# Three PSUM banks for the block products, and another order of weight sums, input sums, splits and norms

## The chip, the cores and the metric

One core of a Trainium2 chip runs the program. The metric is the device time of one execution in microseconds (us); lower is better. Engines in the text: PE (TensorE, matrix products), PEld (its weight loads), DVE (VectorE), ACT (ScalarE), POOL (GpSimd), SP (the engine that issues most of the DMAs).

## The reference

A layer norm of x, 32-head attention on it (q, k, v from one 512 x 1536 matrix), a squared-ReLU feed-forward whose SiLU gates the attention's output, and a residual. S = 2048 tokens, D = 512, 32 heads of 16, F = 1792, all float32.

```python
def _A_ref(x, wqkv, wo):
    qkv = (x @ wqkv).reshape(B, S, 3, H, Dh)      # -> q, k, v per head
    p = softmax(q @ k.T * Dh ** -0.5)
    return (p @ v).reshape(B, S, D) @ wo

def _B_ref(x, w1, b1, w2, b2):
    h = relu(x @ w1 + b1) ** 2
    return h @ w2 + b2

xn = layernorm(x)
out = x + _A_ref(xn, A_wqkv, A_wo) * silu(_B_ref(xn, B_w1, B_b1, B_w2, B_b2))
```

## The kernel before

The order of all work is written by hand: each engine runs its instructions in the order in which the program issues them, and a tile framework adds the semaphore waits that the tiles' reads and writes call for.

**Stages.** The tokens come in four chunks of 512 (`NC = 4`). The first part of the span, up to about 176 us, makes v, k and q of all chunks; the rest is one long loop over heads and key blocks (scores on L381, exponentials on L385, values on L699, the feed-forward's products on L429 between them). This case is about the first part.

**Precision.** Each float32 operand is split in two parts of a reduced format, high (a cast) and low (the difference, L104 or L298). A product takes three of the four combinations: high-high, high-low, low-high.

**A chunk.** `norm` (L159) normalizes two token tiles at a time: statistics (L166, L172), a square root on ACT (L176), three small DVE operations (L179 to L181), and the normalization (L186). `transposes` (L214) turns a chunk on PE (L201) into two PSUM tiles S0 and S1, ACT copies the high part (L205), DVE makes the low part (L211), and four sums of input quarters follow (L228, L231). `split_sums` (L234) splits those four sums: 0 and 3 with POOL, 1 and 2 with DVE. Then four value tiles of 12 matmuls each (`linear`, L111) are copied by ACT into `vt` (L655), and four groups g of keys and queries follow.

**Chunk 0** makes keys and queries directly (`keyquery`, L273: 12 matmuls of 512 columns into a rotating S tile, an ACT cast L98, a DVE subtraction L104, one DMA). Between its groups stand the four weight sums (`weight_sum`, L286, on DVE, L290, in place in the raw weight tiles) and their splits (`split_weight_sum`, L293: a cast on ACT, L296, and two subtractions on POOL, L298).

**Chunks 1 to 3** make keys and queries of a group together, as a 2 x 2 block product with seven products in place of eight (`fast_keyquery`, L314). A product is six matmuls of 256 columns (L324). The seven use input quarters, the four input sums (x sums, tags u0, u1, y0, y1), weights, and the four weight sums. ACT copies the first product out as r (L331) into `tmp`, which lies in the tile QA1; that tile held the raw weights from which weight sum 3 is made. DVE adds the products up (L327), and ACT and DVE and POOL make high and low parts (L343, L351, L352, L354). Two DMAs on SP write keys and queries. Before, the products go round four banks:

```python
    four_banks = t([128, 2, 512], FT, "S2")
    four_banks = [t([128, 512], FT, "lin"), four_banks[:, 0], four_banks[:, 1], t([128, 512], FT, "acc")]
```

so banks two and three are halves of one tile, and the value tiles go to them first: `four_banks[(1, 2, 3, 0)[i]]`.

**Chores.** DVE's add in `fast_keyquery` may be followed by one step of a generator, `chores`: the transposes, low parts and input sums of the next chunk, one step behind every third add. The norms of the next chunk run among the value tiles.

**PSUM.** Eight banks: S0, S1, S2 of two banks each, `lin` and `acc`.

Of the kernel before, what the change touches and what calls it, by code (L numbers as in the profile page):

```python
# [24 lines left out]
FT = mybir.dt.float32  # L25
FR = mybir.dt.float32r
I32 = mybir.dt.int32
AF = mybir.ActivationFunctionType
OP = mybir.AluOpType
# [44 lines left out]
def fast_path(tc, sb, ps, env):  # L74
# [7 lines left out]
    dve, act, pool, sp = nc.vector, nc.scalar, nc.gpsimd, nc.sync  # L82
# [3 lines left out]
    def t(shape, dt, tag):  # L86

        cnt[0] += 1
        p = ps if tag in ("S", "S0", "S1", "S2", "lin", "acc") else sb
        if tag in BUFS:  # L90
            turn[tag] = turn.get(tag, -1) + 1
            n = turn[tag] % BUFS[tag]
            tag = f"{tag}{places[n] if tag == 'S' else n}"
        return p.tile(shape, dt, tag=tag, name=f"{tag}_{cnt[0]}")
# [7 lines left out]
    def split(hi, lo, src, heng, leng):  # L102
        cast(heng, hi, src)
        leng.tensor_tensor(lo, src, hi.bitcast(FT), op=OP.subtract)  # L104
# [9 lines left out]
    def run(gen):  # L114
        for _ in gen:
            pass
# [10 lines left out]
    def load_x(c):  # L127
        for i in range(2):
            a = xload[c, i] = t([128, 2, 512], FT, f"P{4 + 2 * (c == 1) + i}")
            r = c * 512 + i * 256  # L130
            sp.dma_start(a, x[r:r + 256].rearrange("(a p) d -> p a d", p=128))
            if c == i == 0:
                load_w("v", sp, (0,))
# [100 lines left out]
    def split_sums(c, which, eng):  # L234
        for j in which:
            tag = ("u0", "u1", "y0", "y1")[j]
            xs4[j] = t([128, 2, 2, 256], FR, tag)
            split(xs4[j][:, 0], xs4[j][:, 1], xsum[c][j], act, eng)
# [47 lines left out]
    def weight_sum(j):  # L286

        (k0, k1), (q0, q1) = wraw["k"], wraw["q"]
        dst, u, v = ((k0, q0, k0), (q1, q1, k0), (q0, q1, q0), (k1, q1, k1))[j]
        dve.tensor_tensor(dst, u, v, op=OP.subtract)  # L290
        return dst

    def split_weight_sum(j, h, l):  # L293

        src = wraw[("k", "q", "q", "k")[j]][(0, 1, 0, 1)[j]]
        act.copy(h, src)  # L296
        for k in range(2):
            pool.tensor_tensor(l[k], src[:, k], h[:, k].bitcast(FT), op=OP.subtract)  # L298
        ws4[j] = [h[:, 0], h[:, 1]], l
# [12 lines left out]
        return lambda p, k: wsp[which][p][2 * j + k][:, s]  # L312

    def fast_keyquery(c, g, banks, chores, tags, tmp):  # L314
        one, two, three, four = (b[:, :256] for b in banks)
        r, u2, u3 = (tmp[:, j] for j in range(3))
        kk, qq = (t([128, 2, 512], FT, tag) for tag in tags)
        khi, qhi, klo, qlo = (e[:, p].bitcast(FR) for p in range(2) for e in (kk, qq))

        def product(dst, xn, wn, more=False):  # L320
            xp, wp = x_part(c, xn), w_part(wn, g)
            todo = [(k, a, b) for a, b in ((0, 0), (0, 1), (1, 0)) for k in range(2)]
            for n, (k, a, b) in enumerate(todo):
                mm(dst, wp(a, k), xp(b, k), start=n == 0 and not more, stop=n == 5, skip_group_check=True)  # L324

        def add(dst, u, v, op=OP.add):
            dve.tensor_tensor(dst, u, v, op=op)  # L327
            next(chores, None)

        product(one, (0, 0), ("k", 0))  # L330
        act.copy(r, one)  # L331
        product(two, 2, 2)
        add(u2, two, r)
        product(three, 3, 3)
        add(u3, three, u2)
        product(four, 1, 1)
        add(qq[:, 1, 256:], four, u3)
        if (c, g) == (3, 3):
            turn["S"] = -1
            first = [scores(0, p) for p in range(2)]  # L340
            exps(0, 0, first[0])
        product(one, (0, 1), ("k", 1), more=True)
        act.copy(khi[:, :256], one)  # L343
        if (c, g) == (3, 3):
            exps(0, 1, first[1])
        add(klo[:, :256], one, kk[:, 0, :256], OP.subtract)
        product(two, (1, 1), 4)
        add(kk[:, 1, 256:], u3, two, OP.subtract)
        product(four, 4, ("q", 1), more=True)
        add(qq[:, 1, :256], four, u2)  # L350
        act.copy(khi[:, 256:], kk[:, 1, 256:])  # L351
        act.copy(qhi, qq[:, 1])  # L352
        add(klo[:, 256:], kk[:, 1, 256:], kk[:, 0, 256:], OP.subtract)
        pool.tensor_tensor(qlo, qq[:, 1], qq[:, 0], op=OP.subtract)  # L354
        sp.dma_start(kdram[g][c // 2][:, :, 512 * (c % 2):512 * (c % 2) + 512], kk)
        sp.dma_start(qdram[g][c], qq)
# [26 lines left out]
    def exps(i, p, src):  # L383
        if src is not None:
            act.activation(ptile[i, p], src, AF.Exp, scale=SCALE)  # L385
# [184 lines left out]
    parts = [norm(0, (0,)), norm(0, (1,)), norm(0, (2, 3))]  # L570
# [28 lines left out]
    def chain(*gens):  # L599
        for g in gens:  # L600
            yield from g

    parts = chain(norm(1, (0, 1)), norm(1, (2, 3)))
# [5 lines left out]
    for g in range(4):  # L609
        if g == 1:  # L610
            bp = t([128, 14], FT, "acc")
            nc.tensor.transpose(bp, b1raw, ident[:14, :14])
            dve.tensor_copy(b1t, bp)
        if g == 3:
            prep = transposes(1)
            for _ in range(3):
                next(prep)
            save_xT(1)
        for which in "kq":
            keyquery(0, g, which, ("lin", "acc")[which == "q"] if g == 3 else "S")  # L620
            next(parts, None)
            if (g, which) == (1, "q"):
                weight_sum(0)
                a = t([128, 2, 2, 512], FR, "KA2")
                split_weight_sum(0, a[:, 0], [a[:, 1, k] for k in range(2)])
            if (g, which) == (2, "k"):
                weight_sum(2)
                weight_sum(1)
                split_weight_sum(1, t([128, 2, 512], FR, "gl"), [t([128, 512], FR, "ou") for _ in range(2)])
            if (g, which) == (2, "q"):  # L630
                weight_sum(3)
        if g == 0:
            load_x(2)
    h, l = (t([128, 2, 512], FR, f"P{6 + p}") for p in range(2))
    split_weight_sum(2, h, [l[:, 0], l[:, 1]])
    run(prep)

    four_banks = t([128, 2, 512], FT, "S2")
    four_banks = [t([128, 512], FT, "lin"), four_banks[:, 0], four_banks[:, 1], t([128, 512], FT, "acc")]
    tmp = t([128, 4, 256], FT, "QA1")  # L640
    for c in range(1, NC):
        split_sums(c, (1, 2), dve)
        split_sums(c, (0, 3), pool)
        if c == 1:
            h, l = (t([128, 2, 512], FR, f"h{p}0") for p in "hl")
            split_weight_sum(3, h, [l[:, 0], l[:, 1]])
        parts = chain(norm(c + 1, (0, 1)), norm(c + 1, (2, 3))) if c < 3 else iter(())
        if c == 3:
            turn["KA"] = 2
            load_ka(0, 0)  # L650
            load_qa(0, 0)
        for i in range(4):
            pv = four_banks[(1, 2, 3, 0)[i]]
            run(linear(pv, lambda p, k: xpart(c, p, k)[:, 128 * i:128 * i + 128], lambda p, k: wsp["v"][p][k]))
            act.copy(vt[:, 4 * c + i, :H * 17].rearrange("p (h e) -> p h e", e=17)[:, :, :DH],  # L655
                     pv.rearrange("p (h e) -> p h e", e=DH))
            for _ in range(2 if i < 2 else 1):
                next(parts, None)
        run(parts)
        if c == 3:  # L660
            act.activation(t([128, 1], FT, "warm"), eps, AF.Exp)
            for _ in range(2):
                load_piece()
        prep = iter(())
        for g in range(4):
            if g == 1 and c < 3:
                prep = transposes(c + 1)
                next(prep)
                if c == 1:
                    load_x(3)  # L670
            if g == 1 and c == 3:
                split_piece(act)
            slow = (next(prep, None) if n % 3 == 2 else None for n in range(6))
            tags = [(f"P{2 * (g % 2)}", f"P{2 * (g % 2) + 1}"), ("P2", "P3"), ("P0", "P1"), ("P4", "P5"), ("T0", "T1")][
                g + 1 if c == 3 else 0]

            fast_keyquery(c, g, four_banks, slow, tags, tmp)
        run(prep)
        if c == 1:
            save_xT(2)  # L680
# [10 lines left out]
    acc = [None]  # L691
# [221 lines left out]
    for n in range(TURNS):  # L913
        i = 4 * n
# [44 lines left out]
        if n == TURNS - 1:  # L959
            two = t([128, 2, 512], FT, "S")  # L960
# [17 lines left out]
    ou = t([128, 512], FT, "P0")  # L978
# [3 lines left out]
    h, l = t([128, 512], FR, "wf1h0"), t([128, 512], FR, "wf1l0")  # L982
# [160 lines left out]
```

## Time and profile before

| | |
|---|---|
| Median of 3 runs | 1294.94 us (1293.67 to 1295.03) |
| The profiled execution's own time | 1293.84 us |
| Its span | 1292.1 us |
| PE busy | 1256.8 us (97%) |
| ACT busy | 1061.9 us (82%) |
| DVE busy | 713.8 us (55%) |
| POOL busy | 294.8 us (23%) |
| Mean granted PE clock of the run | 0.992 |
| Span behind 176.36 us | 1115.74 us, of which PE is busy 1105.97 |

The span is the profiled part of one execution; the 1.7 us between it and that execution's time lie around it. In the lines of the profile "L324" is line 324 of the kernel, "S<-u,gl" is the written tile and the read ones (buffer numbers left out), "x6" the number of instructions merged, the first number the start in us from the span's start and the second the length. A bracket such as [0.59 <-DVE QA L327] says how long the engine was idle before and which instruction ended that. Ends of PE's matmuls are modelled: the next matmul starts before the last one's end, so a pause in the order of starts is some 0.15 us longer than the idle time in the bracket.

### The profile page before, as it was taken

What the parts mean: (1) busy time and instruction counts of PE and PEld (TensorE: products, weight loads), DVE (VectorE), ACT (ScalarE), POOL (GpSimd) and SP (SyncE); (2) the same over time, 40 slices, a digit from 0 to 9 for tenths busy, and PEclk for the clock granted to TensorE, in tenths of its full rate; (3) what the DMA queues carried; (4) which work ended last, traced back from release to release, by engine and by line L of the source; (5) the groups of instructions that cost most, each with busy time, mean ns of one, the idle gap of its engine ahead of it and who ended that gap; (6) DMA issues with size and microseconds to landing.
All of it is one profiled execution on the core that took longest, in us unless ns stands there. A gap on an engine that the chain in (4) does not pass through costs nothing.

```text
span 1292.1 us, 25643 instructions
## 1 busy us (share of the span) xinstructions
PE 1256.8 (97%) x10245; PEld 725.3 (56%) x10245; DVE 713.8 (55%) x1140; ACT 1061.9 (82%) x1172; POOL 294.8 (23%) x176
## 2 busy tenths in 40 slices
PE   9688899999999999999999999999999999999997
PEld 7587765555555555555555555555555555545554
DVE  5656455556555655555555545455554545566655
ACT  4323368989899889899998989899988999998884
POOL 5312222212020222222112212120221222321212
PEclk9899999999999999999999999999999999999999
DMA  7523552313123323222422332132323232463445
GB/s 269 196 105 158 207 184 59 102 43 91 47 87 120 106 75 91 57 78 58 156 75 58 108 86 64 42 101 106 95 72 90 59 91 58 135 215 111 138 140 122
DMA packets 84944, 137.37 MB, mean 106 GB/s; under 512 B 26058, under 2 KB 40408, under 8 KB 83284
## 3 DMA queue, kind: packets, MB, share of 16 engines
q1 hardware_dynamic: 81668, 126.25, 30.9%
q0 software_dynamic: 2720, 8.65, 2.3%
q8 instruction: 81, 1.33, 0.4%
q10 hardware_dynamic: 432, 0.79, 0.2%
q14 instruction: 43, 0.35, 0.1%
HBM read 94.24 MB, written 41.41 MB: 105 GB/s over the span
## 4 chain that ended last, share of the span: by engine, by line
PE 91%; DVE 3%; ACT 3%; issue 1%; DMA 1%; POOL 0%; SPq 0%; ACTq 0%; DVEq 0%
PE acc L699 35%; PE spare L429 23%; PE S L381 16%; PE lin L381 8%; PE S L324 2%; PE acc L324 1%; PE spare L449 1%; PE lin L324 1%; PE S L111 1%; PE lin L111 1%; PE acc L111 1%; DMA P<-in_A_x_dram 1%; PE spare L438 0%; DVE QA L327 0%; POOL hl L104 0%
## 5 line engine op out<-in xcount | busy, mean ns | idle before, releaser
L385 ACT ACTIVATE P<-S 128x1024 f32<-128x1024 f32 x768 | 739.6, 1020 | 69.8 <-PE S L381 67.0
L404 DVE COPY P<-lin 128x512 f32<-128x512 f32 x512 | 353.9, 691 | 464.5 <-PE lin L381 426.1
L699 PE MATMUL acc<-P,vt 128*32 128x512 f32 x4096 | 466.0, 595 | 0.0
L381 PE MATMUL S<-QA,KA 64*128 64x512 f32 x1536 | 344.6, 423 | 0.1
L385 ACT ACTIVATE P<-P 128x1024 f32<-128x1024 f32 x256 | 271.3, 1060 | 32.0 <-DVE P L404 31.3
L699 PEld LDWEIGHTS acc<-P,vt 128*32 128x32 f32 x4096 | 120.1, 110 | 263.7 <-issue 263.7
L381 PEld LDWEIGHTS S<-QA,KA 64*128 64x128 f32 x1536 | 163.8, 183 | 176.0 <-ACT P L385 140.1
L381 PE MATMUL lin<-QA,KA 64*128 64x512 f32 x512 | 214.2, 418 | 0.5 <-DVE P L404 0.2
L104 POOL TENSOR_TENSOR wf1l<-wr,wf1h 128x1024 fp32r<-128x1024 f32 x28 | 66.7, 2384 | 281.0 <-DVE wf1h L100 136.1
L104 POOL TENSOR_TENSOR hl<-T,hh 128x1024 fp32r<-128x1024 f32 x28 | 67.7, 2416 | 242.2 <-DVE hh L100 165.9
L104 POOL TENSOR_TENSOR wf2l<-wr,wf2h 128x1024 fp32r<-128x1024 f32 x28 | 66.7, 2382 | 205.1 <-PE acc L699 138.9
L429 PE MATMUL spare<-xl,wf1h 64*128 64x512 f32 x440 | 109.1, 391 | 0.0
L381 PEld LDWEIGHTS lin<-QA,KA 64*128 64x128 f32 x512 | 94.2, 184 | 26.6 <-DVE P L404 3.6
L429 PE MATMUL spare<-wf2l,hh 64*128 64x512 f32 x400 | 97.1, 391 | 0.0
L429 PE MATMUL spare<-xh,wf1l 64*128 64x512 f32 x504 | 96.0, 391 | 0.0
L429 PE MATMUL spare<-xh,wf1h 64*128 64x512 f32 x504 | 95.6, 390 | 0.0
L429 PE MATMUL spare<-wf2h,hh 64*128 64x512 f32 x448 | 85.6, 390 | 0.0
L429 PE MATMUL spare<-wf2h,hl 64*128 64x512 f32 x416 | 81.0, 391 | 0.0
L429 PEld LDWEIGHTS spare<-xh,wf1h 64*128 64x128 f32 x504 | 59.9, 184 | 9.4
L429 PEld LDWEIGHTS spare<-xh,wf1l 64*128 64x128 f32 x504 | 60.0, 185 | 7.8
L429 PEld LDWEIGHTS spare<-xl,wf1h 64*128 64x128 f32 x440 | 62.4, 185 | 0.8
L429 PEld LDWEIGHTS spare<-wf2h,hh 64*128 64x128 f32 x448 | 53.9, 184 | 8.1
(288 smaller groups left out, 1210.6 us busy)
## 6 DMA issues: line engine op xcount, KB each, us to landing
wr<-in_B_w_dram SPq DMA_DIRECT2D x56, 512.0 KB
KA<-kd SPq DMA_DIRECT2D x64, 256.0 KB
QA<-qd SPq DMA_DIRECT2D x128, 128.0 KB
kd<-P SPq DMA_DIRECT2D x15, 512.0 KB
qd<-P SPq DMA_DIRECT2D x15, 512.0 KB
u<-ud SPq DMA_DIRECT2D x15, 512.0 KB
P<-in_A_x_dram SPq DMA_DIRECT2D x8, 512.0 KB
xd<-KA SPq DMA_DIRECT2D x4, 1024.0 KB
```

Source lines behind the costliest of these rows:

```text
L104: leng.tensor_tensor(lo, src, hi.bitcast(FT), op=OP.subtract)
L111: mm(dst, lhs(a, k), rhs(b, k), start=n == 0, stop=n == len(todo) - 1)
L324: mm(dst, wp(a, k), xp(b, k), start=n == 0 and not more, stop=n == 5, skip_group_check=True)
L381: mm(dst, k[r, p, 128 * (kb % 8):128 * (kb % 8) + 128], q[r, p], start=True, stop=True)
L385: act.activation(ptile[i, p], src, AF.Exp, scale=SCALE)
L404: dve.tensor_copy(ptile[i, p][:, hp], single)
L429: mm(bank, self.lhs(a, k)[r], self.rhs(b, k)[r], start=n == 0 and self.at[other] == 0, stop=n == len(self.todo[half]) - 1 and self.at[othe ...
L449: mm(bank[:, c], self.lhs(a, k)[r], self.rhs(b, k)[r, c], start=False, stop=False)
L699: mm(acc[0][32 * j:32 * j + 32], vt[:, kb, o:o + 32], ptile[i, j // 2][:, j % 2], start=kb == 0, stop=kb == NK - 1)
```

## The change

Three things change in the program; the arithmetic is the same.

- **Banks.** `fast_keyquery` takes three banks, `lin`, `acc` and one bank of S2, each a tile of its own, in place of four. The seven products go one, two, three, two, one, three, two (before: one, two, three, four, one, two, four). The four value tiles go to banks three, two, one, three.
- **Weight sums and their splits.** Sum 0 stays behind group 1 of chunk 0. Sum 2 and the split of sum 0 come behind the queries of group 2, the rest of the transposes (`run(prep)`) before the split of sum 2, then sums 1 and 3. The splits of sums 1 and 3 come behind the first and the second value tile of chunk 1.
- **Input sums and norms.** The input sums of a chunk are split behind its first (1 and 2, DVE) and second (0 and 3, POOL) value tile, not ahead of all four. A norm step runs behind every value tile, and the steps left over run as chores in the first group. The transposes of the next chunk begin at group 2, not 1, and a chore stands behind every second add, not every third. With them the load of input chunk 3 (`load_x(3)`) is issued at group 2 of chunk 1.

```diff
--- before.py
+++ after.py
@@ -312,7 +312,7 @@
         return lambda p, k: wsp[which][p][2 * j + k][:, s]
 
     def fast_keyquery(c, g, banks, chores, tags, tmp):
-        one, two, three, four = (b[:, :256] for b in banks)
+        one, two, three = (b[:, :256] for b in banks)
         r, u2, u3 = (tmp[:, j] for j in range(3))
         kk, qq = (t([128, 2, 512], FT, tag) for tag in tags)
         khi, qhi, klo, qlo = (e[:, p].bitcast(FR) for p in range(2) for e in (kk, qq))
@@ -333,8 +333,8 @@
         add(u2, two, r)
         product(three, 3, 3)
         add(u3, three, u2)
-        product(four, 1, 1)
-        add(qq[:, 1, 256:], four, u3)
+        product(two, 1, 1)
+        add(qq[:, 1, 256:], two, u3)
         if (c, g) == (3, 3):
             turn["S"] = -1
             first = [scores(0, p) for p in range(2)]
@@ -344,10 +344,10 @@
         if (c, g) == (3, 3):
             exps(0, 1, first[1])
         add(klo[:, :256], one, kk[:, 0, :256], OP.subtract)
-        product(two, (1, 1), 4)
-        add(kk[:, 1, 256:], u3, two, OP.subtract)
-        product(four, 4, ("q", 1), more=True)
-        add(qq[:, 1, :256], four, u2)
+        product(three, (1, 1), 4)
+        add(kk[:, 1, 256:], u3, three, OP.subtract)
+        product(two, 4, ("q", 1), more=True)
+        add(qq[:, 1, :256], two, u2)
         act.copy(khi[:, 256:], kk[:, 1, 256:])
         act.copy(qhi, qq[:, 1])
         add(klo[:, 256:], kk[:, 1, 256:], kk[:, 0, 256:], OP.subtract)
@@ -621,60 +621,57 @@
             next(parts, None)
             if (g, which) == (1, "q"):
                 weight_sum(0)
+            if (g, which) == (2, "q"):
+                weight_sum(2)
                 a = t([128, 2, 2, 512], FR, "KA2")
                 split_weight_sum(0, a[:, 0], [a[:, 1, k] for k in range(2)])
-            if (g, which) == (2, "k"):
-                weight_sum(2)
-                weight_sum(1)
-                split_weight_sum(1, t([128, 2, 512], FR, "gl"), [t([128, 512], FR, "ou") for _ in range(2)])
-            if (g, which) == (2, "q"):
-                weight_sum(3)
         if g == 0:
             load_x(2)
+    run(prep)
     h, l = (t([128, 2, 512], FR, f"P{6 + p}") for p in range(2))
     split_weight_sum(2, h, [l[:, 0], l[:, 1]])
-    run(prep)
-
-    four_banks = t([128, 2, 512], FT, "S2")
-    four_banks = [t([128, 512], FT, "lin"), four_banks[:, 0], four_banks[:, 1], t([128, 512], FT, "acc")]
+    weight_sum(1)
+    weight_sum(3)
+
+    banks = [t([128, 512], FT, tag) for tag in ("lin", "acc", "S2")]
     tmp = t([128, 4, 256], FT, "QA1")
     for c in range(1, NC):
-        split_sums(c, (1, 2), dve)
-        split_sums(c, (0, 3), pool)
-        if c == 1:
-            h, l = (t([128, 2, 512], FR, f"h{p}0") for p in "hl")
-            split_weight_sum(3, h, [l[:, 0], l[:, 1]])
         parts = chain(norm(c + 1, (0, 1)), norm(c + 1, (2, 3))) if c < 3 else iter(())
+        prep = iter(())
         if c == 3:
             turn["KA"] = 2
             load_ka(0, 0)
             load_qa(0, 0)
         for i in range(4):
-            pv = four_banks[(1, 2, 3, 0)[i]]
+            pv = banks[(2, 1, 0)[i % 3]]
             run(linear(pv, lambda p, k: xpart(c, p, k)[:, 128 * i:128 * i + 128], lambda p, k: wsp["v"][p][k]))
             act.copy(vt[:, 4 * c + i, :H * 17].rearrange("p (h e) -> p h e", e=17)[:, :, :DH],
                      pv.rearrange("p (h e) -> p h e", e=DH))
-            for _ in range(2 if i < 2 else 1):
-                next(parts, None)
-        run(parts)
+            if i < 2:
+                split_sums(c, ((1, 2), (0, 3))[i], (dve, pool)[i])
+                if c == 1 and i == 0:
+                    split_weight_sum(1, t([128, 2, 512], FR, "gl"), [t([128, 512], FR, "ou") for _ in range(2)])
+                if c == 1 and i == 1:
+                    h, l = (t([128, 2, 512], FR, f"h{p}0") for p in "hl")
+                    split_weight_sum(3, h, [l[:, 0], l[:, 1]])
+            next(parts, None)
         if c == 3:
             act.activation(t([128, 1], FT, "warm"), eps, AF.Exp)
             for _ in range(2):
                 load_piece()
-        prep = iter(())
         for g in range(4):
-            if g == 1 and c < 3:
+            if g == 2 and c < 3:
+                run(parts)
                 prep = transposes(c + 1)
                 next(prep)
                 if c == 1:
                     load_x(3)
             if g == 1 and c == 3:
                 split_piece(act)
-            slow = (next(prep, None) if n % 3 == 2 else None for n in range(6))
+            slow = (next(parts, None) or next(prep, None) if n % 2 else None for n in range(6))
             tags = [(f"P{2 * (g % 2)}", f"P{2 * (g % 2) + 1}"), ("P2", "P3"), ("P0", "P1"), ("P4", "P5"), ("T0", "T1")][
                 g + 1 if c == 3 else 0]
-
-            fast_keyquery(c, g, four_banks, slow, tags, tmp)
+            fast_keyquery(c, g, banks, slow, tags, tmp)
         run(prep)
         if c == 1:
             save_xT(2)
```

## The prediction

> **What bounds the kernel now.** I read the page first, then the busy times of stretches of the span, then PE's order of time from 36 to 178 us, and last the other engines at PE's pauses.
>
> ```profile
> span 1292.1 us, 25643 instructions
> PE 1256.8 (97%) x10245; PEld 725.3 (56%) x10245; DVE 713.8 (55%) x1140; ACT 1061.9 (82%) x1172; POOL 294.8 (23%) x176
> ```
>
> ```profile
> 39.69:54.94 15.25, 9.20 (x42) 7.77 (x41) 9.66 (x13) 4.04 (x5) 4.52 (x3) 0.78 0.47 187
> 54.94:99.43 44.49, 36.60 (x233) 32.52 (x232) 27.66 (x60) 16.07 (x32) 11.93 (x9) 0.92 0.34 125
> 99.43:138.04 38.61, 34.32 (x235) 30.87 (x233) 25.19 (x58) 13.91 (x30) 8.29 (x6) 1.00 0.42 164
> 138.04:176.36 38.32, 33.51 (x223) 29.45 (x222) 14.79 (x31) 15.30 (x30) 10.58 (x7) 1.00 0.54 192
> ```
>
> The second fence is four stretches: length, then busy time of PE, PEld, DVE, ACT and POOL, PE's granted clock, DMA share, GB/s. They are the hand-over from chunk 0 and then chunks 1, 2 and 3. PE is busy 97% of the span, but only 82 to 89% of each chunk and 60% of the hand-over, at a clock of 0.78. The change touches only these 137 us; the 1,116 us behind them are PE's own and move with them.
>
> PE there, with what ended its pauses:
>
> ```profile
> 46.78 1.97 PE L201 MATMUL S<-ident,P 128*128 128x128 f32 x8 [6.05 <-DVE P L104]
> ...
> 62.41 2.07 PE L111 MATMUL S<-wf1h,xh 128*128 128x512 f32 x4 [4.60 <-ACT vt L655]
> ...
> 75.25 0.40 PE L324 MATMUL S<-u,ou 128*128 128x256 f32 x2
> 76.23 0.97 PE L324 MATMUL S<-y,P 128*128 128x256 f32 x6 [0.59 <-DVE QA L327]
> ...
> 103.37 1.20 PE L111 MATMUL S<-wf1h,KA 128*128 128x512 f32 x4 [0.96 <-ACT vt L655]
> ...
> 160.08 0.97 PE L324 MATMUL S<-y,P 128*128 128x256 f32 x6 [1.45 <-DVE QA L327]
> ```
>
> ```profile
> 44.47 1.04 ACT L296 CAST gl<-wr 128x1024 fp32r<-128x1024 f32 x1 [5.88 <-DVE wr L290]
> 45.42 0.58 ACT L98 CAST P<-S 128x512 fp32r<-128x512 f32 x1
> ```
>
> The 6.05 us pause waits for the last S bank of chunk 0, whose eviction (ACT at 45.42) stands behind the cast of weight sum 1, and that behind two sums on DVE. The 4.60 us pause is value tile 1 waiting for ACT to copy value tile 0 out of the other half of S2, behind six casts. The 0.59 is block product three waiting for DVE's read of product two: two halves of one tile, two banks.
>
> **The change, part by part.** I replay PE's order with the durations of these rows: a value tile 2.73 us (12 matmuls, 52.22 to 54.94), a product 0.72 (6 matmuls), DVE L327 0.42, ACT L331/L343 0.37, POOL on 128x512 1.25, weight sum 1.2, its cast 1.05.
>
> *Hand-over.* Two weight sums and two casts go behind the eviction. PE ends query group 2 at 39.85, ACT's cast ends 40.5, DVE's 41.15: the second transposes start near 41.2, not 46.78. The 8 transposes after the pause took 1.62 us and 12 matmuls 3.82 instead of 1.0 and 2.73, as the clock had fallen. Value tile 0 starts at 41.2 + 0.9 + 2 x 2.73 = 47.5, before at 54.94: **gain 7.4**. The sum that stays (2, at 41.1) and the cast of sum 0 lie beside transposes and key/query matmuls.
>
> *Value tiles of chunk 1.* Before, 54.94 to 73.97 = 19.0, with the 4.60 pause, 12 matmuls at half speed (5.24 instead of 2.73) and 0.84 for the last copy. After: 4 x 2.73 = 10.9, in three tiles of their own. But ACT's queue now holds the square root of the norm ahead of the copy of value tile 2, and the root waits for DVE: sums 1 and 3 until 54.7, two splits, two statistics, until 58.8. The copy ends near 59.8, block 0 starts then, not at 58.4. 10.9 + 1.4 = 12.3: **gain 6.7**.
>
> *The first block of chunk 1* is where the moved work collides. r, product one's copy into QA1, now waits for POOL to finish the split of weight sum 3, which reads QA1; before it was done 9 us earlier. POOL has six ops from 54.7 on (sum 1, two input sums, sum 3). DVE has, ahead of its first add, two splits, a norm and two statistics. These rows tell how the two share:
>
> ```profile
> 62.26 1.27 POOL L104 TENSOR_TENSOR y<-T,y 128x512 fp32r<-128x512 f32 x1
> 63.49 2.50 POOL L298 TENSOR_TENSOR hl<-QA,hh 128x512 fp32r<-128x512 f32 x2
> ```
>
> ```profile
> 63.58 1.20 DVE L180 SCALAR_TENSOR_TENSOR rs<-mv,rs 128x2 f32<-128x2 f32 x1
> 64.81 1.20 DVE L181 SCALAR_TENSOR_TENSOR rs<-rs 128x2 f32<-128x2 f32 x1
> ...
> 101.31 1.39 DVE L104 TENSOR_TENSOR u<-T,u 128x512 fp32r<-128x512 f32 x1 [0.32 <-ACT u L98]
> ```
>
> ```profile
> 102.39 1.43 POOL L104 TENSOR_TENSOR u<-T,u 128x512 fp32r<-128x512 f32 x1 [0.25 <-ACT u L98]
> ```
>
> A tiny DVE op (0.16 alone) takes 1.20, the length of the POOL op beside it, and a split of 0.68 takes 1.39. I let them alternate: POOL's ops end at 56.6, 58.5, 59.8, 61.0, 62.6, 64.0, DVE's three small ops fall between the last four, two normalizations and two statistics follow, and add u2 runs at 66.1 to 66.5. Product four needs it; its turn is 59.85 + 3 x 0.72 = 62.0. Wait 4.5. If each ran at its own length instead, u2 would end at 62.3 against a turn of 60.6: 1.7, and block 0 would start at 58.4. I take 4.5 and keep 1.7. The Trainium skill (SBUF — State Buffer, Who interferes with whom) has a DVE op with two SBUF inputs and a reading GpSimd op exclude each other for a whole instruction; by it the wait is the 4.5, and the rows at 63.58 and 64.81 agree with 1.20.
>
> Behind a wait of 4.5 the clock may fall: after pauses of 6.05 and 4.60 PE ran at half speed, losing 2.5 after the second; after 1.45 (160.08) it lost nothing. I take 1.2, ends 0 and 2.5. The Trainium skill (TensorE: Matmul & The Clock Gate, What's actually happening) has the clock halve after an idle window of about 3.4 us and stay so about as long, which would cost an estimated 1.7.
>
> *Blocks, three banks.* PE's order is one two three two one three two. A block loses 0.73 before (75.49 to 76.23), 10.35 over all twelve (nine of 0.73, and 1.04, 1.08, 1.61). Now three has its own tile and runs during add u2, and product four reuses two after one product: 0.72 of work over 0.74 of round trip, nothing left. But where DVE has another op ahead of the block's last adds, the next block's product two waits. Chunks 1 and 2, second block: the normalization (0.2 + 3 x 0.2 + 1.0 = 1.7) now stands after the add to klo; the last add ends 2.0 behind the block, its bank is wanted at 0.72: 1.3. Third block: transposes' two ACT copies (1.92) keep r late: 0.4. Fourth: one 0.65 us op: 0.24. Chunk 3: the table load (1.28) and r delay product four by 0.9; the split piece's cast (1.04) by 0.8. So after: chunk 1 4.5 + 1.2 + 1.3 + 0.4 + 0.24 = 7.6, chunk 2 1.9, chunk 3 1.7, together 11.3: **loss 0.9**.
>
> *Value tiles of chunks 2 and 3*: 103.37 - 102.25 = 1.1 and 0.84 (block one behind the last copy) go away, twice: **gain 3.9**. Input splits and norms there lie beside 10.9 us of matmuls; u2 is free at 12.0, wanted at 12.4.
>
> *Queues.* The load of input chunk 3 goes on SP one block later, behind both writes of chunk 1's second block (near 75); it is 1 MB and wanted near 90. A MB read takes 6.0 us by the KA load's row in the page's issues, so it is hidden by 9 us; without that cover it costs up to 6. Key/query writes keep their order; a P pair comes back after two blocks, 10.2 us, now instead of 11.7.
>
> Sum: 7.4 + 6.7 - 0.9 + 3.9 = **17.1**. Span 1292.1 becomes 1275.0, that execution's time 1293.84 becomes 1276.7. The median shown is 1.1 above it: **1277.8**.
>
> **Rivals.** *No collision:* POOL and DVE fall apart in time. First-block wait 1.7, clock held, block 0 at 58.4: 2.8 + 1.2 + 1.4 = 5.4 better, 1272.4. For it: POOL idles 15 us before the block in the old trace; against: the same rows as above. *Worse collision:* POOL ops at 1.75 (as at 103.78) six times, +3.0; full clock loss, +1.3; the second blocks' small ops meet POOL, 2 x 2.3: 8.9 worse, 1286.7. *Halves still tied* (the change doesn't do what it says): three keeps its 0.73; 10.35 stays on top of the new 11.3, 1288.1. The changed kernel's list of instructions shows no wait of product three on DVE from the second block on, against it. *The ring closes (slower):* one mechanism, every product waits for the eviction of its bank, because DVE's in-order queue runs a full 0.73 late. Each of seven products so hit costs 12 x 0.73 = 8.8. Parts outside the blocks gain 18.0, the old waits 10.35: it decides from 28.4 / 8.8 = 3.2 waiting products per block. All seven: 61.3 - 28.4 = 33 slower, 1328. For it: only one product lies between two uses of bank two. Against: five of seven have two or three between (1.4 to 2.2 us), and DVE is busy 25.19 of 38.61 us.
>
> **How the numbers follow.** Forecast 0.60, no collision 0.17, worse collision 0.12, halves tied 0.05, ring 0.04, something within noise 0.02. The range reaches from below the no-collision case, 1270, to near the worse collision, 1286. 0.2% is 2.6 us, about what runs of this kernel can tell from no change. Faster is all but the last two: 0.94; same 0.02; slower 0.04.
>
> **What would show it.** Right: no pause above 1 us before the second transposes; value tiles back to back; products two and three adjacent; one pause of 2 to 5 us in chunk 1's first block, ended by DVE's add, with POOL's split of sum 3 just before; pauses near 1.3 in second blocks; chunk 3 ending near 159 instead of 176.36. Wrong: half-speed matmuls behind 41 us, or the loop's own length changed by over 2 us.

## The result, and the profile after

Four runs of the changed kernel took 1277.36 to 1277.97 us, median 1277.47; the kernel before took 1294.31 (four runs, 1293.36 to 1295.03). The ratio is 0.9871, 95% interval 0.9854 to 0.9888: 1.3% faster. The profiled span went from 1292.1 to 1275.7 us, 16.4 less; the forecast was 17.1 less and a time of 1277.8. The profiled execution took 1277.50.

Stages, cut where PE starts each (first value tile, first block product, end of the last block), from PE's order of time in both profiles:

| stage | before, us | after, us | gain | forecast gain |
|---|---|---|---|---|
| hand-over, to value tile 0 of chunk 1 | ends 54.94 | ends 47.72 | 7.2 | 7.4 |
| value tiles of chunk 1 | 19.03 | 11.81 | 7.2 | 6.7 |
| blocks of chunk 1 | 25.46 | 30.04 | -4.6 | -4.4 |
| value tiles of chunks 2 and 3 | 26.14 | 22.03 | 4.1 | 3.9 |
| blocks of chunk 2 | 25.54 | 24.90 | 0.6 | 1.35 |
| blocks of chunk 3 | 25.25 | 23.37 | 1.9 | 2.1 |
| the loop behind them | 1115.7 | 1115.8 | -0.1 | 0 |

The forecast gain of a block stage is the old waits of its four blocks less the new ones of the prediction.

The pauses of PE that are left, and three neighbours, from PE's order of time in the changed kernel:

```profile
41.32 1.09 PE L201 MATMUL S<-ident,P 128*128 128x128 f32 x8 [0.57 <-DVE P L104]
...
59.53 0.51 PE L324 MATMUL lin<-xh,wf2h 128*128 128x256 f32 x2 [0.77 <-ACT vt L648]
...
61.06 0.86 PE L324 MATMUL S<-y,P 128*128 128x256 f32 x6
65.66 1.65 PE L324 MATMUL acc<-u,KA 128*128 128x256 f32 x6 [3.74 <-DVE QA L327]
...
80.60 0.99 PE L324 MATMUL acc<-u,KA 128*128 128x256 f32 x6 [0.19 <-DVE QA L327]
...
89.57 1.20 PE L111 MATMUL S<-wf1h,KA 128*128 128x512 f32 x4 [0.42 <-DVE P L327]
...
107.74 0.74 PE L324 MATMUL acc<-u,gl 128*128 128x256 f32 x4 [1.13 <-DVE P L327]
...
139.57 0.96 PE L324 MATMUL acc<-u,KA 128*128 128x256 f32 x6 [0.79 <-DVE QA L327]
```

The 6.05 us hand-over pause is 0.57 and the 4.60 among the value tiles is gone. Product three follows product two at once everywhere. New is the pause of 3.74 in chunk 1's first block, and after it six matmuls take 1.65 us instead of 0.97: half speed.

What was queued ahead of the add that ended it, from the orders of time of DVE, POOL and ACT in the changed kernel:

```profile
59.04 0.17 DVE L178 RECIPROCAL rs<-rs 128x2 f32<-128x2 f32 x1 [0.36 <-ACT rs L176]
59.24 0.42 DVE L179 SCALAR_TENSOR_TENSOR rs<-rs 128x2 f32<-128x2 f32 x1
59.69 1.21 DVE L180 SCALAR_TENSOR_TENSOR rs<-mv,rs 128x2 f32<-128x2 f32 x1
60.94 1.21 DVE L181 SCALAR_TENSOR_TENSOR rs<-rs 128x2 f32<-128x2 f32 x1
62.18 1.91 DVE L186 TENSOR_SCALAR P<-P,mv,rs 128x512 f32<-128x512 f32 x2
64.01 1.27 DVE L166 BATCH_NORM_STATS2 st<-P 128x6 f32<-128x512 f32 x2
65.20 0.40 DVE L327 TENSOR_TENSOR QA<-acc,QA 128x256 f32<-128x256 f32 x1
```

```profile
59.60 1.28 POOL L104 TENSOR_TENSOR y<-T,y 128x512 fp32r<-128x512 f32 x1
60.85 2.49 POOL L298 TENSOR_TENSOR hl<-QA,hh 128x512 fp32r<-128x512 f32 x2
```

```profile
63.37 0.37 ACT L331 COPY QA<-lin 128x256 f32<-128x256 f32 x1 [3.41 <-POOL hl L298]
```

DVE runs from 59.04 to 65.20 without a gap; two of its small operations take about the length of the POOL operation beside them (1.21 against some 1.25, instead of 0.16), and two normalizations take 1.91 instead of 1.00. The copy r (ACT at 63.37) waits for POOL, but is done 1.5 us before DVE comes to the add.

### The profile page after: what moved, and what is told of

It is laid out like the page before. It is cut to its first block, busy times and chain, and to the rows that moved or that the text cites. A ratio compares the mean times of both kernels' runs of the same rounds, so it can differ in the third digit from the quotient of the medians.

```text
span 1275.7 us, 25643 instructions
## 1 busy us (share of the span) xinstructions
PE 1254.7 (98%) x10245; PEld 725.3 (57%) x10245; DVE 712.3 (56%) x1140; ACT 1061.5 (83%) x1172; POOL 293.8 (23%) x176
## 4 chain that ended last, share of the span: by engine, by line
PE 92%; DVE 3%; ACT 2%; issue 1%; DMA 1%; POOL 0%; SPq 0%; ACTq 0%; DVEq 0%
PE acc L696 36%; PE spare L429 23%; PE S L381 16%; PE lin L381 8%; PE acc L324 2%; PE S L111 2%; PE spare L449 1%; PE lin L324 1%; PE S L324 1%; ACT P L385 1%; PE lin L111 1%; PE acc L111 1%; DMA KA<-in_A_wqkv_dram 1%; PE spare L438 0%; POOL hl L104 0%
## 5 line engine op out<-in xcount | busy, mean ns | idle before, releaser
L104 POOL TENSOR_TENSOR hl<-T,hh 128x1024 fp32r<-128x1024 f32 x28 | 67.6, 2415 | 241.6 <-DVE hh L100 138.7
```

## Experiments

Five of the eight experiments have one execution (those without "median" in the table), and for these the span alone is a poor yardstick: the loop behind the first stages differs by a microsecond or so from execution to execution (spans of the kernel before on one chip: 1292.3 to 1294.1). So next to each kernel's time stands a mark near the end of the changed stages: the start of the last two matmuls of chunk 3's last product, in the profiled execution.

| kernel | mark, us | span, us | time, us |
|---|---|---|---|
| before | 176.03 | 1292.1 | 1294.31 median |
| after | 159.54 | 1275.7 | 1277.47 median |
| three banks alone (e1) | 161.10 | 1276.9 | 1278.64 median |
| new order alone (e2) | 171.59 | 1288.3 | 1289.10 median |
| copies r in QA0 (e3) | 159.61 | 1276.5 | 1278.23 |
| the same, chunk 1's norm as chores (e5) | 156.62 | 1273.2 | 1275.09 |
| weight work earlier (e6) | 154.31 | 1270.4 | 1272.22 |
| fillers in the pause (e9) | 158.32 | 1274.5 | 1276.36 |
| small waits (e7) | 155.43 | 1272.0 | 1273.77 |
| weight work and small waits (e8) | 148.91 | 1265.4 | 1267.17 median |

**The three banks alone**, on the kernel before; sums, splits and norms where they were:

```diff
-        product(four, 1, 1)
+        product(two, 1, 1)
...
+    banks = [t([128, 512], FT, tag) for tag in ("lin", "acc", "S2")]
...
-            pv = four_banks[(1, 2, 3, 0)[i]]
+            pv = banks[(2, 1, 0)[i % 3]]
...
```

> The kernel before with the three banks alone (ring one two three two one three two, value tiles in three tiles); all sums, splits and norms in the old order. Theory (banks and order are two effects that share a stretch): hand-over pause of 6 us stays, value tiles of chunk 1 lose their 4.6 us pause, but the last copies and the add u2 wait for the second norm until about 70.9; each block loses its 0.73. Span 16 to 17 us under before, near 1275.7, as short as the whole change. Rival (the order is what the gain needs): under 10 us gained, span over 1282.

Measured: median 1278.64, ratio to before 0.9875 (0.9859 to 0.9892). PE's pauses in chunk 0 and chunk 1, from its order of time in this kernel:

```profile
46.82 1.97 PE L201 MATMUL S<-ident,P 128*128 128x128 f32 x8 [6.07 <-DVE P L104]
...
69.66 0.98 PE L324 MATMUL S<-y,P 128*128 128x256 f32 x6 [2.06 <-ACT vt L654]
...
71.35 1.65 PE L324 MATMUL acc<-u,KA 128*128 128x256 f32 x6 [0.71 <-DVE QA L327]
```

The 6.07 us pause is there, yet the mark moves by 14.9 of the change's 16.5 us. So the other half of the change adds only 1.6 on top of the banks, and by the times (0.9875 against 0.9871) no more than the intervals leave open. Stage by stage against this kernel, the changed one is 7.4 ahead at the hand-over (47.72 against 55.13) and gives back 0.9 in chunk 1's value tiles (11.81 against 10.88), 2.7 in chunk 1's blocks (30.04 against 27.33) and 2.2 in chunk 2's (24.90 against 22.74).

**The new order alone**, the changed kernel with the four banks of before:

> The changed kernel with the four banks of before; sums, splits, norms and chores in the new order. Theory: the hand-over gains its 7.2 us, then product three (not four) waits for add u2 in chunk 1's first block, and all blocks and value tiles keep the waits on halves of S2: span 1285.8, some 6.5 under before. Rival (order carries most of it): span under 1280.

Measured: median 1289.10, ratio 0.9954 (0.9937 to 0.9970); spans 1286.6 to 1288.3, the profiled one the longest. From the table of waits of this kernel (who waited for whom, us in total, times, longest), the row of the block products on the halves of S2:

```profile
PE S L324 <- DVE QA L327: 12.3, 12, 3.5
```

PE's order of time behind the longest of these waits:

```profile
65.66 0.97 PE L324 MATMUL S<-y,P 128*128 128x256 f32 x6 [3.55 <-DVE QA L327]
66.47 1.24 PE L324 MATMUL acc<-u,KA 128*128 128x256 f32 x6
67.50 0.63 PE L324 MATMUL lin<-xh,wf2h 128*128 128x256 f32 x2
...
70.83 0.40 PE L324 MATMUL lin<-xh,wf2h 128*128 128x256 f32 x2
```

By the medians the gain is 5.9, near what was expected; the profiled execution, the longest, gains 4.4 at the mark. All twelve blocks wait for add u2 at product three; without the longest, the eleven others have 8.8 us of idle time, or 0.8 each, where the twelve of the kernel before have 8.4, or 0.7 each. And a slow stretch was not counted: from 65.66 to 70.83 PE does 30 matmuls in 5.17, where 12 at full speed take 1.51 (73.65 to 75.16), so 30 take 3.8: 1.4 lost. The two halves of the change give 14.9 + 4.4 = 19.3 singly and 16.5 together.

**Does r's wait for POOL make the pause?** `tmp` lies in QA0 in chunk 1, so r waits for no split:

```diff
-    tmp = t([128, 4, 256], FT, "QA1")
...
+        if c < 3:
+            tmp = t([128, 4, 256], FT, f"QA{min(c - 1, 1)}")
```

> The changed kernel; in chunks 1 and 2 the tile tmp lies where it waits for nothing of weight sum 3 (QA0 in chunk 1, QA1 from chunk 2 on). Theory (DVE's own queue, held up by POOL op for op, ends last): add u2 still runs near 65.2, pause of 3.7 us stays, span 1275.5 +- 0.7. Rival (the copy of r waiting for POOL decides): pause down to 2 us or less, span down by 2 to 4 us.

Measured: span 1276.5. From the orders of time of ACT and PE of this kernel:

```profile
60.61 0.37 ACT L331 COPY QA<-lin 128x256 f32<-128x256 f32 x1 [0.65 <-PE lin L324]
```

```profile
65.64 1.65 PE L324 MATMUL acc<-u,KA 128*128 128x256 f32 x6 [3.73 <-DVE QA L327]
```

r comes 2.8 us earlier and the pause is the same to 0.01: DVE's queue decides, the wait for POOL on QA1 lay beside it. The mark is that of the change (159.61 against 159.54); the span of this one execution is 0.3 above the expected range.

**The norm taken out of the way**, as above and chunk 1's norm steps as chores:

```diff
-            next(parts, None)
+            if c > 1:
+                next(parts, None)
```

> As e3_tmp, and chunk 1 runs its norm steps as chores of the first two groups, none among the value tiles. Theory (norm and statistics ahead of u2 in DVE's queue, and r): block 0 starts near 58.6, product four has no pause over 0.3, product six waits about 0.7 for the split of sum 3, PE keeps its clock; 6 us gained at the end of block 0, 1 to 2.5 given back behind groups 0 and 1 where the norm now stands: span 1271 to 1273. Rival (clock falls for another reason than the pause): matmuls of the first block's end still at half speed, span above 1274.

Measured: span 1273.2. PE's pauses in chunk 1, from its order of time:

```profile
63.40 0.38 PE L324 MATMUL S<-xh,hl 128*128 128x256 f32 x1 [0.41 <-POOL hl L298]
...
68.44 0.97 PE L324 MATMUL acc<-u,KA 128*128 128x256 f32 x6 [1.73 <-DVE QA L327]
...
74.41 1.06 PE L201 MATMUL S<-ident,P 128*128 128x128 f32 x8 [1.96 <-issue]
```

The first block runs without the pause of product four and at full speed; the norm then stands in the second block's way (1.73). Two normalizations, beside a POOL subtraction each time, take 2.06 there and 2.04 ahead of the second transposes, which start 1.96 late; for these the profile names no releaser, so that the norm holds them up is read from the order alone. The mark is 2.9 better than the change's; the span is 0.2 above what was expected.

**The weight work taken out of the way**, the norm left where the change has it:

```diff
+            if (g, which) == (3, "k"):
+                weight_sum(1)
+                weight_sum(3)
...
     run(prep)
-    split_weight_sum(2, h, [l[:, 0], l[:, 1]])
-    weight_sum(1)
-    weight_sum(3)
+    split_weight_sum(1, t([128, 2, 512], FR, "gl"), [t([128, 512], FR, "ou") for _ in range(2)])
+    h, l = (t([128, 2, 512], FR, f"h{p}0") for p in "hl")
+    split_weight_sum(3, h, [l[:, 0], l[:, 1]])
...
```

(the split of sum 2 goes ahead of group 3's keys, and those of sums 1 and 3 leave the loop over the value tiles)

> The changed kernel; weight sums 1 and 3 behind the keys of chunk 0's last group, the split of sum 2 ahead of them, those of sums 1 and 3 ahead of the value tiles. Theory (work of weight sums standing beside chunk 1's first block makes its pause): block 0 starts near 58.6, pause of product four 0.5 (ends 0 to 1.5), PE keeps its clock, block 0 ends near 64.3 instead of 70.95, the second block's wait for the norm comes back (1.2): span 1270 (1269 to 1271.5). Rival (the norm alone makes the pause): pause still over 2.5, span over 1274.

Measured: span 1270.4; the mark is 5.2 under the change's. From PE's order of time:

```profile
61.63 0.96 PE L324 MATMUL acc<-u,KA 128*128 128x256 f32 x6 [0.65 <-DVE QA L327]
...
66.59 0.74 PE L324 MATMUL acc<-u,gl 128*128 128x256 f32 x4 [1.12 <-DVE P L327]
```

From the orders of time of DVE and POOL in this kernel:

```profile
58.66 0.16 DVE L180 SCALAR_TENSOR_TENSOR rs<-mv,rs 128x2 f32<-128x2 f32 x1
59.05 1.01 DVE L186 TENSOR_SCALAR P<-P,mv,rs 128x512 f32<-128x512 f32 x2
61.17 0.41 DVE L327 TENSOR_TENSOR QA<-acc,QA 128x256 f32<-128x256 f32 x1
```

```profile
57.33 1.29 POOL L104 TENSOR_TENSOR y<-T,y 128x512 fp32r<-128x512 f32 x1
```

The same norm, on the same queue, now costs 0.65 instead of 3.74: POOL is done by 58.6 and DVE's small operations run at 0.16 again. The add comes 4.0 earlier than in the changed kernel (61.17 against 65.20). Of this 1.1 is an earlier start (the norm's operations begin at 57.98, not 59.04), as DVE's own weight sums have moved too; the other 3.0 is what the same operations save without POOL beside them. And the second block's wait of 1.1, which the change did not show in chunk 1, is there.

**Is the slow stretch PE's own idling?** 18 matmuls whose result nobody reads fill the pause (the trace lists two instructions for each):

```diff
+        if (c, g) == (1, 0):
+            fill = t([128, 512], FT, "S0")
+            for _ in range(18):
+                mm(fill[:, :128], ident, ident, start=True, stop=True)
         product(two, 1, 1)
```

> The changed kernel with 18 matmuls of 128 columns, whose result nobody reads, in chunk 1's first block ahead of product four, where PE pauses. Theory (idle PE loses its clock, and the slow stretch hides the second block's wait): product four still starts near 65.7, the rest of the block at full speed, block 0 ends 2.3 earlier, near 68.6; 1.0 of it is given back in the second block: span 1274.4 (1273.9 to 1275). Rival (matmuls are slow for DVE's and POOL's sake): granted clock and block end unchanged, span 1275.7.

Measured: span 1274.5. PE's order of time in this kernel, then the stretch from 66 to 71 us (its length, busy time of PE, PEld, DVE, ACT, POOL, granted clock, DMA share, GB/s), first here and then in the changed kernel:

```profile
61.72 4.18 PE L339 MATMUL S<-ident 128*128 128x128 f32 x36
65.66 0.97 PE L324 MATMUL acc<-u,KA 128*128 128x256 f32 x6
...
70.62 0.74 PE L324 MATMUL acc<-u,gl 128*128 128x256 f32 x4 [1.13 <-DVE P L327]
```

```profile
66.00:71.00 5.00, 3.87 (x33) 3.67 (x32) 3.63 (x14) 1.41 (x4) 0.00 (x0) 1.00 0.02 5
```

```profile
66.00:71.00 5.00, 5.00 (x25) 5.00 (x25) 2.54 (x11) 0.67 (x2) 0.00 (x0) 0.50 0.00 2
```

Product four starts at the same 65.66 with DVE and POOL as before, but the granted clock is 1.00, not 0.50, and the block ends at 68.61 instead of 70.95. Of these 2.3 us the second block's wait takes 1.1 back: the mark is 1.2 earlier. So PE's idling, and not the work of DVE and POOL, brought the slow stretch, and the slow stretch hid the next wait.

**The small waits**, the first block left as it is: value tiles in banks one, three, two, three; the norm's last step cut in three; the table load of Exp behind the third value tile of chunk 3; the split piece's cast behind r:

```diff
...
-            pv = banks[(2, 1, 0)[i % 3]]
+            pv = banks[(0, 2, 1, 2)[i]]
...
+            if c == 3 and i == 2:
+                act.activation(t([128, 1], FT, "warm"), eps, AF.Exp)
...
+                slow = (split_piece(act) if n == 1 else None for n in range(6))
...
```

> The changed kernel; value tiles in banks one, three, two, three; the last step of the norm cut in three chores; the table of Exp loaded behind the third value tile of chunk 3; the split piece's cast a chore behind r. Theory: the waits of 0.57 (twice), 1.3 (chunk 2's second block), 0.9 and 0.75 (chunk 3) go, chunk 1's first block stays as it is: 3.7 us less, span 1272.0 (1271 to 1273). Rival (they were covered by the next wait): less than 1.5 us.

Measured: span 1272.0, the mark 4.1 earlier than the change's. Behind chunk 1's first block PE's order of time shows only two idle times before the loop, 0.18 and 0.22.

**The weight work and the small waits together:**

> e6_weights and e7_small together. Theory (they add up): span 1265 (1264 to 1267), time 1266.7, 0.990 to 0.992 of the changed kernel and 0.978 of the kernel before. Rival (the gains overlap): span 1268 or more.

Measured: median 1267.17 (1266.73 to 1267.88), ratio to before 0.9791 (0.9778 to 0.9804). The two gains at the mark are 5.2 + 4.1 = 9.3; together they give 10.6. The extra 1.3 is near the second block's wait of chunk 1 (1.12), which the weight work alone brings up and the small waits remove. The stretch from chunk 1's first block to the end of chunk 3's last, first here and then in the changed kernel, columns as above:

```profile
58.50:149.25 90.75, 89.45 (x639) 82.87 (x637) 55.61 (x136) 38.23 (x78) 21.71 (x16) 1.00 0.53 198
```

```profile
59.53:159.90 100.37, 92.73 (x638) 85.60 (x638) 59.19 (x137) 37.95 (x78) 25.46 (x20) 0.97 0.49 179
```

For the same work PE is busy 89.45 of 90.75 us at full clock instead of 92.73 of 100.37 at 0.97: this version is faster than both kernels, and little but the work itself is left to take in this stretch.

## Why the prediction was right, step by step

The mechanisms hold, and most sizes with them. That the totals agree so closely is in part luck, in two places named below.

- *Hand-over.* 7.4 forecast, 7.2 measured. The second transposes start at 41.32 (forecast 41.2). Experiment e1 keeps the old order there and keeps the pause (6.07), and e2 has the new order with the old banks and 0.57: shown.
- *Value tiles of chunk 1.* 6.7 forecast, 7.2 measured. Block 0 starts at 59.53 (59.85), behind the copy of value tile 2, which stands behind the square root on ACT as forecast; the wait was 0.9, not 1.4. Either half of the change alone takes most of the old 19.03 away: the stage is 10.88 with the banks alone (e1) and 12.71 with the order alone (e2), which is one reason why the halves do not add up.
- *The first block of chunk 1.* Forecast: DVE and POOL take turns, add u2 at 66.1, product four waits 4.5. Measured: u2 at 65.20, product four 3.86 late (61.80 to 65.66). The mechanism is shown from both sides: without the norm there is no pause (e5), and without POOL's work beside it the same norm leaves 0.65 (e6). In detail it differs: two small operations were stretched, not three, and POOL was done at 63.34, not 64.0, while the normalizations were stretched too (1.91 instead of 1.00), which the forecast did not have. That r's wait on QA1 was named beside it did no harm, but it decided nothing (e3).
- *The clock.* 1.2 forecast between ends of 0 and 2.5. Gross the slow stretch costs 2.3, net 1.2 (e9). The forecast charged the clock and the second block's wait (1.3) separately; in chunk 1 the second hid behind the first. The stage of chunk 1's blocks agrees to 0.2 by luck: the pause was 0.6 shorter than forecast, the slow stretch 1.1 longer, the second block's wait of 1.3 did not show, and a wait of 0.57 that was missed (below) is counted in it.
- *Three banks.* Product three waits no more, and product four, one product behind, is on time to 0.02 where nothing else stands in DVE's queue. Second block of chunk 2: 1.3 forecast (the terms in its bracket add up to 1.8, not 1.7; the rows from 105.24 to 106.94 give 1.70); its product starts at 107.74 where 106.45 was its turn. Third blocks: 0.4 forecast, about 0.3 measured. Fourth: 0.24 forecast, about 0.2. Chunk 3: 0.9 and 0.8 forecast, measured 0.9 and 0.8 between starts.
- *A wait that was missed.* "Value tiles back to back" failed at value tile 0 of chunks 2 and 3: it goes to bank three, whose last read, an add to keys, stands behind a chore (0.42 at 89.57; 0.57 between starts). Twice 0.57 is 1.1 us, which with the smaller errors above makes 16.4 of 17.1. Taking bank one first removes it (e7). The forecast of the time came closer than that of the span, again by luck: it added 1.1 for a median above the profiled execution, and after the change the two lie together (1277.47 and 1277.50).
- *Rivals.* No collision (1272.4): e6 brought the state about by moving the work, and its one run took 1272.22, but with other terms (a pause of 0.65, not 1.7, and the second block's wait of 1.12 in full). The 15 us for which POOL idles in the old trace, named in its favour, run from 66.0 to 81.25, and only 8 of them lie ahead of the block (73.97). Worse collision did not come: POOL's last four operations took some 1.25 each, not 1.75. Halves still tied is out in the changed kernel, and e2 shows what they cost. The ring did not close: with bank two's turn this tight, no block lost more to it than it had lost before, save where a norm, a table load or a cast stood ahead.
- *Signs.* Half-speed matmuls behind 41 us, named as a sign of being wrong, did not come at the hand-over (eight transposes in 1.09 from 41.32); those from 65.66 on were in the sum.
- *Input chunk 3's load* was issued at 79.47 and its first statistics ran at 94.98 without a wait for it: hidden, as forecast.

## What to carry to other kernels

Two halves of one tile wait for each other even in different banks; here three banks in tiles of their own did better than four of which two shared a tile, and this half of the change alone moved the mark by 14.9 of the 16.5 us. Work taken off one wait lands in another queue: before moving it, list what stands ahead of the next block's first add on every engine, and which DVE and POOL operations will run side by side. After a long pause, count the slow stretch that follows and what it hides; filling the idle time can be worth less than it looks, because the next wait then shows.

## What the hardware showed that was not expected

PE's clock did not follow the length of the last pause alone. After 3.73 and 3.74 the next matmuls ran at half speed at once (six in 1.65); after 3.55 (the new order alone) six took 0.97, full speed, and the fall came with the next six (1.24). A pause of 2.06 and, one product later, one of 0.71 (the banks alone) brought half speed too, while 1.73 and 1.96 six microseconds apart (e5) did not.

The granted clock of short stretches shows why. In stretches of 0.1 us it reads 1.00 or 0.50, with another value only in the stretch of a change. So a mean over 5 us tells how long the clock was halved: 0.85 is 1.5 us, 0.66 is 3.4. First two stretches of the changed kernel, on either side of the one from 66 to 71 us above (0.50), then two of the new order alone, columns as above:

```profile
61.00:66.00 5.00, 1.26 (x9) 1.06 (x9) 4.86 (x7) 0.37 (x1) 2.34 (x2) 0.85 0.00 0
71.00:76.00 5.00, 5.00 (x40) 4.83 (x40) 2.97 (x9) 1.60 (x4) 1.28 (x1) 0.97 0.49 193
```

```profile
61.00:66.00 5.00, 1.45 (x13) 1.25 (x11) 4.57 (x6) 0.37 (x1) 2.35 (x2) 1.00 0.00 0
66.00:71.00 5.00, 5.00 (x32) 5.00 (x31) 2.44 (x10) 0.67 (x2) 0.00 (x0) 0.66 0.01 2
```

The changed kernel has 1.5 + 5.0 + 0.3 = 6.8 us at half clock, the other 3.4. By stretches of 0.1 us:

| kernel | PE idle | clock halved | for |
|---|---|---|---|
| before, hand-over | 40.7 to 46.8 | 43.7 to 50.5 | 6.8 |
| before, value tiles of chunk 1 | 57.8 to 62.4 | 60.8 to 67.6 | 6.8 |
| after, chunk 1's first block | 61.9 to 65.7 | 64.5 to 71.3 | 6.8 |
| new order alone (e2) | 62.1 to 65.7 | 66.8 to 70.2 | 3.4 |
| three banks alone (e1), first block | 67.6 to 69.7, 70.6 to 71.4 | 71.3 to 74.7 | 3.4 |

In the changed kernel the clock fell while PE was still idle, 1.2 us before its matmuls went on, so they met half speed at once and had it for 5.6 us. In the other two it fell when PE went on (e1) or 1.1 us later (e2).

All lengths are one or two times 3.4 us. The Trainium skill (TensorE: Matmul & The Clock Gate, What's actually happening) describes a free-running window of about 3.4 us. The lengths agree with it. Only the 1.7 that the prediction estimated from the Trainium skill was too little for the changed kernel (2.3), as the halved clock lasted two such windows there and not one.

If the windows end where the clock changes (an inference), each fall in the table came at the end of one in which PE had idled for 2.3 us (e2) to 3.0 (before), and the clock came back at the end of the first in which PE never paused. In e5 no stretch of 3.4 us holds more than 1.96 of idle time, and nothing fell. How much idle time is enough, between these 1.96 and 2.3, no run here shows.
